# Block-sparse attention and a gated MLP in one kernel: weight parts taken straight from float32, a second weight scaled by halves, merged output products, a new order

## The chip, the core and the metric

One Trainium2 chip, one of its cores. The metric is the device time of one execution in microseconds (us). Engines are named as in the profile: PE (TensorE; PEld is its weight loads), DVE (VectorE), ACT (ScalarE), POOL (GpSimd), SP (SyncE, which here only issues DMAs).

## What is computed

```python
scores = (q @ k.T) / sqrt(64)            # 4 batches, 8 heads, 768 tokens, head size 64
mask   = block neighbours, first and last block of 32 tokens, 3 sampled blocks per block row
attn   = softmax(where(mask, scores, -1e9)) @ v
x      = attn as [3072, 512]
h      = x @ w_in                        # 512 x 2048
g      = h * tanh(softplus(h))
out    = g @ w_out                       # 2048 x 512, float32
```

The two weights arrive as 64-bit floats; the kernel loads them as pairs of 32-bit words and rebuilds float32 from them on DVE ("decoding"). Products are made from 16-bit parts: a number is a high part plus a low part, and of the four products of two such numbers three are kept.

## The kernel before

**Attention.** A batch has 13 jobs: 2 dense ones (the first and the last block row, all keys) and 11 with two block rows each. `attend` records a job: scores S on PE, row maxima on DVE (`mx`), exponentials on ACT (`pt`), transposes T on PE, their parts (`pp`), the products O with v (`o`), division by the row sums on DVE (`xs`), a transpose (`tx`) and the parts of x (`xh`, `xl`). Keys are gathered by POOL and ACT (`kg`), values by DMA from a copy in DRAM (`vg`, SP's queue). Batch 0 is computed in float32, batches 1 to 3 in 16-bit parts. For those `o_fn` (L781) makes, per half of the heads and per 128 keys, twelve matmuls with 32 columns of weights, four beside each other in four column strips: `hi` times v's high part with a column of ones (65 columns), `hi` times v's low part (64), `lo` times v's high part (65), all added into the same place.

**Weights.** w_in comes in eight pieces of 1 MB (`load_i`, ring `wr` of 3 buffers, SP's queue). DVE decodes a piece into the place of its later parts in `wi` (L889, L892, L895); PE multiplies it with itself for the sums of squares (`gram`, L365); from these a power of two is taken as scale (`add_root`). `split_i` (L934) then makes a scaled float32 copy `wt_i` (POOL, ACT or DVE), its high part (ACT) and its low part (POOL, once DVE). The value `gsc`, needed by every h, wants all eight pieces (`scales_w`). w_out comes in 16 pieces of 0.5 MB in the ring `raw`; it has one scale from one gram over all 16 pieces (`scale_o`, 64 matmuls into a bank of the ring `y`), and `parts_o` (L979) makes a copy and two parts of each piece.

**MLP.** For each of 12 tiles of 256 tokens `moe_h` makes h in 16 pieces of 12 matmuls (L1033), `moe_g` the activation on ACT, DVE and POOL, `moe_y` the output in 16 pieces of 6 matmuls (L1093): for each half m of the tile's tokens eight pieces, summed in the one bank of the ring `y`, then scaled into `ys` (L1104 on ACT or L1106 on DVE) and stored. On the last tile m = 0 uses a bank of the ring `h`.

**Order.** Every operation is recorded with `add(engine, duration, ..., key=...)`. `Plan.emit` then writes all engines' programs from these durations, the rings' sizes and the keys: the earliest possible operation goes first, ties by key; the lists START and RES in `pace` hold a job's scores back in favour of the MLP. Up to the tenth job the planner fills the PE gaps that it expects with matmuls on zeros (`zeros`, L868). At run time each engine works through its own fixed list and waits for semaphores.

Of the kernel before, what the change touches and what calls it, by code (L numbers as in the profile page):

```python
# [9 lines left out]
F32 = mybir.dt.float32  # L10
# [10 lines left out]
SQ = 32  # L21
# [5 lines left out]
             xs=2, hs=3, us=3, g=4, ys=1, kt=1, q=2, ssk=2, ssv=2, ssq=2, sck=2, scv=2, scq=2, iv=2, ns=3, ws=2,  # L27
# [158 lines left out]
def attn_mish_kernel(ctx: ExitStack, tc: tile.TileContext, qT, kT, v, sampled, blocks, w_in, w_out, out):  # L186
# [48 lines left out]
    iv_o = const.tile([P, 1], F32, name="iv_o")  # L235
    sc_o = const.tile([P, 1], F32, name="sc_o")
# [4 lines left out]
    gox = const.tile([P, 1], F32, name="gox")  # L241
    hsc = const.tile([P, B], F32, name="hsc")
    osc = const.tile([P, B], F32, name="osc")
# [123 lines left out]
    def add_gram(key, srcs, keys, ring, out, w, new_, cls):  # L367
# [7 lines left out]
        for n, k in enumerate(keys):  # L375
            add("PE", 0.45 if ring == "y" else 0.8, lambda n=n: fn(n), r=[k], w=[kg], new=[(ring, kg)] if n == 0 else (),
                key=cls - 106, lat=0.25)
# [4 lines left out]
        add("DVE", 0.4, diag, r=[kg], w=w, new=new_, key=cls + 5)  # L382
# [20 lines left out]
    def add_root(key, ss, fn, r, after, w, new, cls, n=1, apart=False):  # L403

        add("PE", 0.3 * n, lambda: root_pe(key, ss(), apart), r=r, w=[key], new=[("t", key)], key=cls + 56, lat=0.3)
        add("DVE", 0.65, fn, port=2, r=[key, *after], w=w, new=new, key=cls + 3)

    def load32(what, j):
# [4 lines left out]
        def fn():  # L413
# [5 lines left out]
            key=-5, lat=1.8, kind=("dma", 4.4 if what == "k" else 1.5, 1))  # L419

    def load(b, what, js, ring="raw", after=()):
# [3 lines left out]
        def fn():  # L425
# [12 lines left out]
            new=[(ring, key) for key in keys], key=(-5 if b == 0 else 0) + (0 if b == 0 else 1), lat=1.8,  # L438
            kind=("dma", 1.5 * n, n))

    def sums(b, what, j, cls):
# [7 lines left out]
        add("ACT", 1.28, fn, r=[("raw", what, b, j)], w=[key], new=[(f"ss{what}", key)] if first else (), key=cls + 47 + (19 if b == 0 else 17))  # L449

    def scales(b, what, j, cls):
# [4 lines left out]
        def fn():  # L456
# [14 lines left out]
        add_root(kp, lambda: tl[ks][:, 0:1] if q else tl[ks], fn, [ks], [("sc", "k", b, 0)] if q else [], [key] + ([("ns", b, j)] if q else []),  # L471
                 [(f"sc{what}", key)] + ([("ns", ("ns", b, j))] if q else []), cls, 1 if q else NTT)

    def parts(b, what, j, cls):
# [32 lines left out]
        if what == "v":  # L507
            add("POOL", 0.5, ends, w=[("ends",) + key], r=[kr], new=[("raw", key)], use=[key], key=cls + 2)
# [3 lines left out]
            use=use + ([key] if what != "k" else []), key=cls + 7)  # L512
        add("DVE", 1.27, lo, port=True, r=[kr, ks, kh], w=[key, ("done",) + key], use=use, key=cls - 8)

    def copy_v(j):
# [26 lines left out]
    def globals_(b):  # L542
# [5 lines left out]
        for n in range(NKG):  # L548
            add("POOL", 1.0, lambda n=n: fn(n), r=KT3(b), w=[("kg", n)], use=[("kt", b)], port=2, key=-14)

    def globals_v(b, n):
# [3 lines left out]
        add("SP", 0.9, fn, r=VD3(b), w=[("vg", n)], key=2, lat=1.8, kind=("dma", 0.5, 2))  # L555
# [19 lines left out]
    def gather_k(su):  # L575
# [12 lines left out]
        add("POOL", 1.3, lambda: fn("POOL"), r=KT3(b) + ["off"], w=[("kg", n)], use=[("kt", b)], port=2, key=53 + (7 if b == 0 else 14),  # L588
            also=[("ACT", 1.6 if exact(b) else 1.9, lambda: fn("ACT"))])
        if su["whole"]:  # L590
            add("DVE", 0.36, lambda: nc.vector.tensor_copy(
                out=kgs[n][:, :, 0:WK], in_=tl["kt", b][:, :, (qb - 1) * BS:(qb + 2) * BS]),
                r=KT3(b), w=[("kw", n)], use=[("kt", b)], port=True, key=4)

    def gather_v(su):
# [15 lines left out]
        add("SP", 2.7, fn, r=VD3(b) + ["off", "z"], w=[("vg", n)], key=-18 + (-24 if b == 0 else 0), lat=1.8, kind=("dma", 1.1, NR + 1 + (a0 > 0) + (a1 < WK)))  # L611

    def fetch_dense(su):
# [11 lines left out]
        for j in T3:  # L625
# [3 lines left out]
                key=-3 + (35 if b == 0 else 1), lat=1.8, kind=("dma", 1.7, 1))  # L629
# [32 lines left out]
    def attend(job):  # L662
# [9 lines left out]
        def s_fn():  # L672
# [17 lines left out]
            use=[("kt", b)], key=-39 + (-21 if b == 0 else 20), lat=0.25, kind=("S", i))  # L690
# [12 lines left out]
        add("DVE", 2.6 if dense else 1.27, mx_fn, r=[ks] + (k2 if dense else []), w=[kmx], new=[("mx", kmx)], key=-3.5 + (-1 if b == 0 else -10))  # L703
# [4 lines left out]
        def nb_fn(eng):  # L708
# [9 lines left out]
            new=[("nb", ("nb", i))], key=45.5 + (0 if b == 0 else -20), also=[("DVE", 0.35 * len(wq), lambda: nb_fn("DVE"))])  # L718
# [16 lines left out]
        for n in range(2):  # L735
            add("ACT", 1.7 if dense and n == 0 else 1.15, lambda n=n: ex_fn(n),
                r=[kmx, ("nb", i), ks] + (k2 if dense else []) + NS,
                w=[("p", i, n)], new=[("pt", k) for k in kps] if n == 0 else (), use=kps, key=-1.5 + (-3 if b == 0 else 7))
# [30 lines left out]
        for j in range(nt):  # L769
            kj = ("t", i, j)  # L770
            add("PE", 0.62 if exact(b) else 0.48, lambda j=j: t_fn(j), r=[("p", i, j // 2 if dense else j)], w=[kj, "t in order"], new=[("t", kj)], use=kps,
                key=-8 + (-40 if b == 0 else 24), lat=0.25, kind=("T", i))
            kpp = ("pp", i, j)
            if exact(b):
                add("ACT", 0.62, lambda j=j: pp_fn(j, "ACT"), r=[kj], w=[("ph", i, j), ("pl", i, j)], use=[kpp],
                    new=[("pp", kpp)], key=-9.5, also=[("DVE", 0.72, lambda j=j: pp_fn(j, "DVE"))])
                continue
            add("ACT", 0.62, lambda j=j: ph_fn(j), r=[kj], w=[("ph", i, j)], new=[("pp", kpp)], use=[kpp], key=1.5)
            add("DVE", 0.72, lambda j=j: pl_fn(j), r=[kj, ("ph", i, j)], w=[("pl", i, j)], use=[kpp], key=11.5)

        def o_fn(j):  # L781
            if j == 0:
                new(ps["o"], "o", ko, [P, 2, 2, D + 2])
            o, w = tl[ko], 0 if dense else j
# [11 lines left out]
            for g in range(2):  # L796
                for k in range(2):
# [514 lines left out]
```

## Time and profile before

| | |
|---|---|
| three timed runs | 766.79 us median (765.13 to 769.03) |
| the profiled execution | 768.72 us, of which the span of the core's work 766.7 us |
| busy in the span | PE 733.4, PEld 507.3, DVE 504.0, ACT 535.8, POOL 230.6 us |
| mean granted TensorE clock | 0.99 of full speed |
| HBM traffic | 79.3 MB read, 12.9 MB written |

The span starts with the first instruction and ends with the last. "Busy" is the time in which at least one instruction of the engine was under way; PE's busy time holds the matmuls on zeros too. In a list of waits the last instruction that released a waiting one is named behind "<-".

### The profile page before, as it was taken

The page shows a single profiled execution, that of the slowest core. Times are in us where ns is not written, and L with a number is a line of the kernel's source. Part 1 is how long each engine was busy: PE and PEld are TensorE (multiplying, and loading weights), DVE is VectorE, ACT ScalarE, POOL GpSimd, SP SyncE. Part 2 cuts the span into 40 slices and gives each one's busy share as a digit, 9 for nine tenths or more (in the row PEclk, how much of TensorE's full clock was granted, in tenths as well). Part 3 has the DMA queues.
Part 4 walks back from the last instruction along what each step waited for, and adds up shares of the span by engine and source line. Part 5 has one row for each costly group of instructions (what it writes and reads, how often), then busy time and mean ns, then how long its engine had stood idle before and what let it go on. Part 6 is the DMA issues. An engine that isn't in the chain of part 4 may idle for free.

```text
span 766.7 us, 28001 instructions
## 1 busy us (share of the span) xinstructions
PE 733.4 (96%) x11905; PEld 507.3 (66%) x11905; DVE 504.0 (66%) x891; ACT 535.8 (70%) x864; POOL 230.6 (30%) x327
## 2 busy tenths in 40 slices
PE   9777898999999999999999999999999999999998
PEld 3554676766677766677767776766776666666663
DVE  3886897887888748859676676777855454425241
ACT  2556787989887867888797678877864655455650
POOL 2363423585645422514340113234522100000000
PEclk9999999999999999999999999999999999999999
DMA  7987768442346533543363336233233221000000
GB/s 263 363 222 219 232 210 230 147 128 87 106 120 168 160 96 110 170 123 105 103 210 97 94 100 200 84 97 101 71 92 90 96 67 48 15 15 15 15 15 27
DMA packets 55904, 94.07 MB, mean 123 GB/s; under 512 B 8035, under 2 KB 18788, under 8 KB 55780
## 3 DMA queue, kind: packets, MB, share of 16 engines
q1 hardware_dynamic: 55584, 92.03, 40.0%
q8 instruction: 93, 1.52, 0.8%
q14 instruction: 31, 0.25, 0.1%
q10 hardware_dynamic: 196, 0.27, 0.1%
HBM read 79.32 MB, written 12.95 MB: 120 GB/s over the span
## 4 chain that ended last, share of the span: by engine, by line
PE 82%; DMA 9%; DVE 4%; issue 2%; SPq 2%; ACT 1%; ACTq 0%; POOL 0%
PE y L1093 31%; PE h L1033 30%; PE t L746 6%; PE o L801 5%; PE s L657 4%; DMA wr<-in_moe_w_in_dram 3%; DMA vg<-vd 3%; PE tx L834 2%; PE o L791 1%; DMA wor<-in_moe_w_out_dram 1%; DMA kt<-in_k_dram 1%; PE s L647 1%; PE zeros L868 1%; DMA raw_q<-in_q_dram 1%; DVE us L1060 1%
## 5 line engine op out<-in xcount | busy, mean ns | idle before, releaser
L1033 PE MATMUL h<-xh,wi 128*128 128x256 f16 x1536 | 285.3, 274 | 0.0
L1093 PE MATMUL y<-wo,g 128*128 128x512 f16 x1152 | 277.7, 379 | 1.5 <-issue 1.5
L1033 PEld LDWEIGHTS <-wi 128*128 128x128 f16 x2304 | 224.7, 99 | 52.4 <-issue 1.5
L1033 PE MATMUL h<-xl,wi 128*128 128x256 f16 x768 | 210.5, 274 | 0.0
L1093 PEld LDWEIGHTS <-g 128*128 128x128 f16 x1152 | 111.0, 98 | 101.2 <-issue 3.2
L585 POOL COPY kg<-kt 128x256 f16 (+1 forms) x222 | 97.6, 485 | 145.6 <-PE s L657 115.8
L1042 ACT ACTIVATE hs<-h,gsc 128x512 f32<-128x512 f32 x96 | 65.6, 683 | 63.7 <-PE h L1033 62.9
L726 ACT ACTIVATE pt<-s,nb,ns 128x256 f32<-128x256 f32 (+1 forms) x208 | 105.7, 580 | 5.1 <-PE t L746 3.1
L1066 DVE SCALAR_TENSOR_TENSOR hs<-us,hs 128x1024 f32<-128x1024 f32 x48 | 59.6, 1242 | 43.1 <-ACT us L1065 43.1
L700 DVE TENSOR_REDUCE mx<-s 128x4 f32<-128x1024 f32 x44 | 53.7, 1221 | 31.5 <-PE s L657 30.1
L1077 POOL TENSOR_TENSOR g<-hs,g 128x1024 f16<-128x1024 f32 x19 | 42.3, 2229 | 98.9 <-ACT g L1072 60.2
L746 PE MATMUL t<-ident,pt 128*128 128x128 f32 x448 | 69.5, 278 | 2.0 <-ACT pt L726 1.7
L1062 POOL TENSOR_TENSOR us<-us 128x1024 f32<-128x1024 f32 x22 | 43.4, 1971 | 74.7 <-DVE us L1060 72.2
L766 DVE SCALAR_TENSOR_TENSOR pp<-t,pp 128x512 f16<-128x512 f32 x84 | 56.1, 681 | 11.6 <-ACT pp L763 11.5
L763 ACT ACTIVATE pp<-t 128x512 f16<-128x512 f32 x84 | 48.3, 590 | 17.7 <-PE t L746 13.7
L746 PEld LDWEIGHTS t<-ident,pt 128*128 128x128 f32 x448 | 50.8, 141 | 13.9 <-ACT pt L726 3.2
L1056 ACT ACTIVATE us<-hs,hsc 128x1024 f32<-128x1024 f32 x48 | 55.1, 1149 | 1.5
L1064 ACT ACTIVATE us<-us 128x1024 f32<-128x1024 f32 x48 | 50.7, 1056 | 4.9 <-POOL us L1062 4.1
L1065 ACT ACTIVATE us<-us 128x1024 f32<-128x1024 f32 x48 | 50.7, 1056 | 0.7
L1060 DVE TENSOR_SCALAR us<-us 128x1024 f32<-128x1024 f32 x48 | 36.5, 760 | 21.7 <-ACT us L1056 21.5
L801 PEld LDWEIGHTS <-pp 128*32 128x32 f16 x4032 | 37.2, 94 | 13.7 <-issue 12.3
L852 ACT ACTIVATE xh<-tx 128x256 f16<-128x256 f32 (+1 forms) x60 | 19.4, 337 | 31.4 <-PE tx L834 24.8
(194 smaller groups left out, 849.7 us busy)
## 6 DMA issues: line engine op xcount, KB each, us to landing
vg<-vd SPq DMA_DIRECT2D x304, 65.0 KB, 2.3
vg<-vd SPq DMA_DIRECT2D x80, 195.0 KB, 2.9
wr<-in_moe_w_in_dram SPq DMA_DIRECT2D x8, 1024.0 KB, 9.2
wor<-in_moe_w_out_dram SPq DMA_DIRECT2D x16, 512.0 KB, 5.0
vd<-v SPq DMA_DIRECT2D x12, 520.0 KB, 3.4
raw_v<-in_v_dram SPq DMA_DIRECT2D x12, 512.0 KB, 5.7
out_dram<-ys SPq DMA_DIRECT2D x24, 256.0 KB, 2.1
raw_q<-in_q_dram SPq DMA_DIRECT2D x9, 512.0 KB, 5.5
```

Source lines behind the costliest of these rows:

```text
L585: nc.gpsimd.tensor_copy(out=dst, in_=src)
L700: nc.vector.tensor_reduce(out=mx.rearrange("p g w -> p (g w)"), in_=tl[ks].rearrange("p g (w k) -> p (g w) k", k=KT), axis=AX.X, op=ALU.max)
L726: ex = lambda o, x, g, w: nc.scalar.activation(out=o, in_=x, func=AF.Exp, bias=nb[:, g, w:w + 1], scale=ns(w)[:, 0:1])
L746: nc.tensor.transpose(t[:, k, g], src, ident)
L766: nc.vector.scalar_tensor_tensor(out=tl["pl", i, j], in0=tl["t", i, j], scalar=PSC, in1=tl["ph", i, j], op0=ALU.mult, op1=ALU.subtract)
L801: nc.tensor.matmul(o[cs, w, g, 0:v1 - v0], p[:, k, g, cs], vt[:, k, 2 * c + g, v0:v1], start=j == 0 and g == 0 and k == 0 and n == 0, stop ...
L1033: nc.tensor.matmul(h[:, f2].rearrange("p (s q) -> p s q", q=BS), wi[:, fp, w, cc, fs], x[:, :, cc], start=f2 == 0 and k == 0, stop=f2 == 1 ...
L1042: nc.scalar.activation(out=tl[kq][:, 2 * (fp % 2):2 * (fp % 2) + 2], in_=tl[kh], func=AF.Copy, scale=gsc[:, fp:fp + 1])
L1056: nc.scalar.activation(out=new(sb, "us", ku, [P, 4, TT]), in_=hs(), func=AF.Exp, scale=hsc[:, b:b + 1])
L1064: add("ACT", 1.07, lambda: nc.scalar.activation(out=us(), in_=us(), func=AF.Ln, bias=1.0), w=[ku], key=10 + (18 if b == 0 else -12))
L1066: add("DVE", 1.32, lambda: nc.vector.scalar_tensor_tensor(out=hs(), in0=us(), scalar=-0.5, in1=hs(), op0=ALU.add, op1=ALU.mult), r=[ku], w ...
L1093: nc.tensor.matmul(tl[ky], tl["g", b, t, k][:, g, f, q], wo[:, fc, w], start=fc == 0 and n == 0, stop=fc == NFC - 1 and n == 2)
```

## The change

It has five parts.

- **w_in.** A decoded piece now goes into a buffer of the rings `us` or `hs` (`at_i`) instead of its place in `wi`. Both parts are made from there: the high part by ACT (or DVE), the low part by one SCALAR_TENSOR_TENSOR on DVE. The scaled copy is gone, and POOL has no part in it.
- **w_out.** Two scales, one for each half of the 16 pieces. The sums of squares come from ACT (`squares`, 16 times) instead of PE's gram. The parts are stored one place on along a chain, so that each is made straight from the decoded piece; only the first high part of a half waits in a buffer.
- **y.** `moe_y` sums each half (two of four k) by itself: 48 sums of 24 matmuls instead of 24 of 48. The first of a pair goes to `ys` scaled, the second is added to it by DVE. `ys` has two buffers. On the last tile the first halves use the ring `h`, the second ones the one bank of `y`.
- **O of batches 1 to 3.** `hi` meets v's high and low part in one matmul of 130 columns for the first three of the four (block row, half of heads) places; the low part's sum lies elsewhere in the bank, is copied out (`xc`) and added on DVE.
- **Sums of k and v squares (batches 1 to 3)** are added on DVE before PE, which then multiplies one column instead of three. **Keys, RES and START** all have other values; v of batch 0 is loaded ahead of k and q.

```diff
-RINGS = dict(... ys=1 ...)
+RINGS = dict(... ys=2 ...)
...
-        add_root(kp, lambda: tl[ks][:, 0:1] if q else tl[ks], fn, ...)
+        three = not q and b == 0
+        if not q and b:
+            add("DVE", 0.2, lambda: nc.vector.tensor_reduce(out=tl[ks][:, 0:1], in_=tl[ks], axis=AX.X, op=ALU.add), r=[], w=[ks], key=cls - 37)
+        add_root(kp, lambda: tl[ks] if three else tl[ks][:, 0:1], fn, ...)
...
-                    for n, (p, v0, v1) in enumerate(((hi, 0, D + 1), (hi, D + 1, 2 * D + 1), (lo, 0, D + 1))):
+                    steps = ((hi, 0, VW, slice(m, m + 5, 4)), (lo, 0, D + 1, m)) if m < 3 else (
+                        (hi, 0, D + 1, m), (hi, D + 1, 2 * D + 1, m), (lo, 0, D + 1, m))
...
+                nc.vector.tensor_tensor(out=xs[:, 0:m], in0=o[:, 0:m, 0:D], in1=xs[:, 0:m], op=ALU.add)
+                nc.vector.tensor_tensor(out=xs[:, 0:m], in0=xs[:, 0:m], in1=rb[:, 0:m].to_broadcast([P, m, D]), op=ALU.mult)
...
+            add("ACT", 0.35, lambda: xc_fn("ACT"), r=[ko], w=[("xc", i)], new=[("xs", ("xs", i))], key=52,
+                also=[("DVE", 0.3, lambda: xc_fn("DVE"))])
...
     def a0_i(k):
-        return wi[:, k].rearrange("p t c f -> p (t c f)").bitcast(F32)
+        return tl["a0", k]
+
+    def at_i(k):
+        ring = ("us", "hs")[k % 2]
+        return [(ring, ("a0", k))], lambda: new(sb, ring, ("a0", k), [P, 4 * TT])
...
-        add("POOL", 1.4, lambda: t_fn("POOL"), r=[ksc, ("wi", k)], w=[kt], new=[("raw", kt)], ...
-        add("ACT", 1.1, lambda: nc.scalar.activation(out=hi, in_=tl[kt], func=AF.Copy), r=[kt], ...
-        add("POOL", 2.1, lambda: nc.gpsimd.tensor_tensor(out=lo, in0=tl[kt], in1=hi, op=ALU.subtract), ...
+        add("ACT", 1.16, lambda: nc.scalar.activation(out=hi, in_=a0_i(k), func=AF.Copy, scale=sc()), r=[ksc, ("wa", k)], ...
+        add("DVE", 1.27, lambda: nc.vector.scalar_tensor_tensor(out=lo, in0=a0_i(k), scalar=sc(), in1=hi, op0=ALU.mult, op1=ALU.subtract), ...
...
-    def scale_o(cls):
-        add_gram(("wo",), [lambda fc=fc: a0_o(fc) for fc in range(NFC)], [("wo", fc) for fc in range(NFC)], "y", ...
+    NHO = 2
+    NFH = NFC // NHO
+    chain = [[h * NFH + (n - 1) % NFH for n in range(NFH)] for h in range(NHO)]
+    before = {c: cs[n - 1] for cs in chain for n, c in enumerate(cs)}
+
+    def wo_of(fc, w):
+        return wo[:, before[fc], 1] if w == 0 else wo[:, fc, 0]
+
+    def scale_o(h, cls):
+        for fc in fcs:
+            add("ACT", 0.65, lambda fc=fc: ss(fc), r=[("oa", fc)], w=[("am1", fc)], ...
...
-        pool = "h" if last and m == 0 else "y"
+        h = k // KH
+        pool = "h" if last and h == 0 else "y"
...
+            if h:
+                nc.vector.scalar_tensor_tensor(out=ys, in0=tl[ky], scalar=sc, in1=ys, op0=ALU.mult, op1=ALU.add)
...
-        ys = [(m, k) for m in range(TT // P) for k in range(NFC // 4)] if prev else []
+        ys = [(m, h * KH + k) for h in range(NHO) for m in range(TT // P) for k in range(KH)] if prev else []
...
-    RES, START = 518, [19, 70, 50, 10, 634, 35, 526, 50, 20, 45, 52, 127, 40, 172, 123, 69, 17, 154]
+    RES, START = 493, [300, 706, 46, 26, 320, 3, 1101, 1150, 300, 903, 90, 104, 101, 108, 1204, 183, 158, 49]
```

Some 60 keys change as well; what they do shows in the order of the engines' programs. Three places of it follow. In the names `h_b_t_n` is piece n of h for batch b, tile t; `o_i`, `s_i`, `t_i`, `tx_i` belong to job i.

PE ahead of the first h, before:

```order
L746 MATMUL t_5_1_1337<-ident_64,pt_5_1261 128x128 x4
...
L365 MATMUL gram_wo_1347<-wo_72 128x128
...
L647 MATMUL s_6_1358<-kt_0_123,q_0_1_167 32x96 x8
L647 MATMUL s_6_1358<-kg0_109,q_0_1_167 32x160 x8
...
L834 MATMUL tx_4_1410<-ident_64,xs_4_1402 128x128 x2
...
L1033 LDWEIGHTS wi_71
L1033 MATMUL h_0_0_0_1444<-xh_0_0_607,wi_71 128x256
```

and now:

```order
L749 MATMUL t_6_1_1464<-ident_64,pt_6_1368 128x128 x4
L650 MATMUL s_7_1478<-kt_0_163,q_0_1_167 32x96 x8
...
L866 MATMUL tx_4_1519<-ident_64,xs_4_1514 128x128 x2
...
L796 MATMUL o_5_1550<-vg0_111,pp_5_0_1227 32x65 x16
...
L796 MATMUL o_5_1550<-vg1_112,pp_5_1_1321 32x65 x16
L749 MATMUL t_7_0_1637<-ident_64,pt_7_1601 128x128 x4
L1087 LDWEIGHTS wi_71
L1087 MATMUL h_0_0_0_1647<-xh_0_0_533,wi_71 128x256
```

The first h now stands behind one job's scores, one job's O and three T groups more; one group of the gram of w_out is gone from there. All zeros stand ahead of it in both programs: 139 before, 160 now.

SP at the loads of w_in (`wr`) and the first gathers of values, before:

```order
L881 DMA wr_4_469<-in_moe_w_in_dram 128x4x512
L554 DMA vg0_111<-vd0_60 32x520 x2
L554 DMA vg1_112<-vd0_60 32x520 x2
L881 DMA wr_5_557<-in_moe_w_in_dram 128x4x512
L604 DMA vg0_111<-vd0_60 64x520
...
L604 DMA vg1_112<-vd0_60 96x520
...
L881 DMA wr_6_763<-in_moe_w_in_dram 128x4x512
L604 DMA vg0_111<-vd0_60 96x520
```

and now:

```order
L913 DMA wr_5_476<-in_moe_w_in_dram 128x4x512
L557 DMA vg0_111<-vd0_60 32x520 x2
L557 DMA vg1_112<-vd0_60 32x520 x2
L913 DMA wr_6_651<-in_moe_w_in_dram 128x4x512
L607 DMA vg0_111<-vd0_60 64x520
...
L607 DMA vg1_112<-vd0_60 96x520
...
L913 DMA wr_7_825<-in_moe_w_in_dram 128x4x512
L607 DMA vg0_111<-vd0_60 96x520
```

Pieces 5, 6 and 7 of w_in each moved ahead by the gathers of one job.

DVE in the last tiles, around the sums of y that go to `ys` (tile 1 of batch 3), before:

```order
L1066 SCALAR_TENSOR_TENSOR hs_3_2_0_15838<-us_3_2_0_15882,hs_3_2_0_15838 128x1024
L1106 TENSOR_SCALAR ys_3_1_0_15981<-y_3_1_0_15810,osc_82 128x512
L1060 TENSOR_SCALAR us_3_2_1_15966<-us_3_2_1_15966 128x1024
L1066 SCALAR_TENSOR_TENSOR hs_3_2_1_15925<-us_3_2_1_15966,hs_3_2_1_15925 128x1024
L1079 TENSOR_TENSOR g_3_2_0_16029<-hs_3_2_0_15838,g_3_2_0_16029 128x1024
L1074 CAST g_3_2_1_16072<-hs_3_2_1_15925 128x1024
```

and now:

```order
L1133 TENSOR_TENSOR g_3_1_3_14847<-hs_3_1_3_14741,g_3_1_3_14847 128x1024
L1168 TENSOR_SCALAR ys_3_1_0_14890<-y_3_1_0_0_14803,osc_82 128x512
L1114 TENSOR_SCALAR us_3_2_0_14875<-us_3_2_0_14875 128x1024
L1120 SCALAR_TENSOR_TENSOR hs_3_2_0_14831<-us_3_2_0_14875,hs_3_2_0_14831 128x1024
L1128 CAST g_3_2_0_14937<-hs_3_2_0_14831 128x1024
L1133 TENSOR_TENSOR g_3_2_0_14937<-hs_3_2_0_14831,g_3_2_0_14937 128x1024
L1168 TENSOR_SCALAR ys_3_1_1_14980<-y_3_1_1_0_14893,osc_82 128x512
```

Each tile's output now empties the bank of `y` four times instead of twice, and each time directly behind a DVE operation on 1024 columns.

## Rows read from the trace of the kernel before

**Rows 1.** The page's busy times of two engines.

```profile
PE 733.4 (96%) x11905; PEld 507.3 (66%) x11905; DVE 504.0 (66%) x891; ACT 535.8 (70%) x864; POOL 230.6 (30%) x327
```

**Rows 2.** Busy time of each engine in three stretches of the span.

```profile
0.00:135.00 135.00, 112.69 (x1906) 75.65 (x1910) 101.09 (x198) 84.04 (x156) 51.33 (x71) 0.96 0.80 249
135.00:300.00 165.00, 164.89 (x2969) 116.77 (x2958) 128.60 (x230) 138.41 (x230) 82.95 (x103) 1.00 0.42 125
...
78.60:141.00 62.40, 55.79 (x1004) 44.19 (x1002) 51.36 (x106) 48.26 (x85) 21.07 (x25) 0.95 0.73 218
```

**Rows 3.** PE's matmuls on zeros, from the groups by form.

```profile
L868 PE MATMUL zeros<-z 128*128 128x512 f16 x139 | 35.7, 400 | 5.6 <-issue 3.9 <-POOL z L863 1.7
```

**Rows 4.** The first h, from PE's timeline.

```profile
81.23 0.27 PE L1033 MATMUL h<-xh,wi 128*128 128x256 f16 x1
```

**Rows 5.** PE's waits in the whole span, the one that the gram of w_out makes.

```profile
PE gram_wo L365 <- DVE wo L895: 3.6, 3, 3.1
```

**Rows 6.** Groups of that gram in PE's timeline.

```profile
90.55 0.39 PE L365 MATMUL gram_wo<-wo 128*128 128x128 bf16 x4
90.78 0.60 PE L746 MATMUL t<-ident,pt 128*128 128x128 f32 x4
...
95.81 0.41 PE L365 MATMUL gram_wo<-wo 128*128 128x128 bf16 x4 [3.06 <-DVE wo L895]
96.05 0.63 PE L746 MATMUL t<-ident,pt 128*128 128x128 f32 x4
```

**Rows 7.** O of a dense and of a two-row job, and what followed, PE's timeline.

```profile
203.11 1.36 PE L801 MATMUL o<-v,pp 128*32 128x65 f16 x144
204.40 0.66 PE L746 MATMUL t<-ident,pt 128*128 128x128 f32 x4
...
219.48 1.01 PE L801 MATMUL o<-vg,pp 128*32 128x65 f16 x96
220.42 0.66 PE L746 MATMUL t<-ident,pt 128*128 128x128 f32 x4
```

**Rows 8.** The last piece of a sum of y, an h piece, the next sum: PE's timeline.

```profile
719.95 1.46 PE L1093 MATMUL y<-wo,g 128*128 128x512 f16 x6
721.25 0.27 PE L1033 MATMUL h<-xh,wi 128*128 128x256 f16 x1
...
722.56 1.46 PE L1093 MATMUL y<-wo,g 128*128 128x512 f16 x6
```

**Rows 9.** The emptying of that bank, DVE's timeline.

```profile
721.45 0.75 DVE L1106 TENSOR_SCALAR ys<-y,osc 128x512 f32<-128x512 f32 x1 [4.60 <-PE y L1093]
```

**Rows 10.** Three columns of squares added on PE, its timeline.

```profile
137.00 0.73 PE L391 MATMUL tp_k<-ss_k,ones 128*128 128x1 f32 x6
```

**Rows 11.** Parts of one job of batch 0 in PE's timeline.

```profile
84.88 0.40 PE L647 MATMUL s<-kt,q 64*32 64x96 f32 x16
...
86.02 0.66 PE L746 MATMUL t<-ident,pt 128*128 128x128 f32 x4
86.61 0.66 PE L791 MATMUL o<-vg,pp 128*32 128x65 f32 x32
87.20 0.66 PE L746 MATMUL t<-ident,pt 128*128 128x128 f32 x4
```

**Rows 12.** DVE's groups by form that the change adds to or takes from.

```profile
L1066 DVE SCALAR_TENSOR_TENSOR hs<-us,hs 128x1024 f32<-128x1024 f32 x48 | 59.6, 1242 | 43.1 <-ACT us L1065 43.1
...
L1060 DVE TENSOR_SCALAR us<-us 128x1024 f32<-128x1024 f32 x48 | 36.5, 760 | 21.7 <-ACT us L1056 21.5
...
L500 DVE SCALAR_TENSOR_TENSOR v<-raw_v,sc_v,v 128x1024 f16<-128x1024 f32 x9 | 11.6, 1304 | 1.5 <-ACT v L496 1.5
```

**Rows 13.** Issues of w_in's pieces 5, 6 and 7 in SP's timeline.

```profile
33.62 0.38 SPq L881 DMA_DIRECT2D wr<-in_moe_w_in_dram  x1
...
44.36 0.45 SPq L881 DMA_DIRECT2D wr<-in_moe_w_in_dram  x1
...
53.21 0.40 SPq L881 DMA_DIRECT2D wr<-in_moe_w_in_dram  x1
```

More of the change, by code (lines that the diff above doesn't have):

```diff
@@ L448, in fn @@
             squares(tl["raw", what, b, j], tl[key][:, k:k + 1])
[L449 removed]
+        add("ACT", 1.28, fn, r=[("raw", what, b, j)], w=[key], new=[(f"ss{what}", key)] if first else (), key=cls + 47 + (41 if b == 0 else -6))
     def scales(b, what, j, cls):
@@ new lines, in parts_o @@
+        add("ACT", 0.65, lambda: h_fn("ACT"), r=[("sc_o", h), ("oa", fc)] + ([] if first else [("wol", before[fc])]),
+            w=[("woh", fc)] + ([kt] if first else []), new=[("raw", kt)] if first else (), key=cls - 31, port=True,
+            also=[("DVE", 0.45, lambda: h_fn("DVE"))])
+        add("DVE", 0.69, lambda: nc.vector.scalar_tensor_tensor(out=lo, in0=a0_o(fc), scalar=sc, in1=to(), op0=ALU.mult, op1=ALU.subtract),
+            r=[("sc_o", h), ("oa", fc), kt if first else ("woh", fc)], w=[("wol", fc)], port=True, key=cls - 32)
@@ L997, in scales_w @@
+        if last:
+            c0 = chain[h][0]
+            src = lambda: tl["wt", c0]
+            add("ACT", 0.6, lambda: nc.scalar.activation(out=wo_of(c0, 0), in_=src(), func=AF.Copy), r=[("wt", c0), ("wol", fc)],
+                w=[("woh", c0)], key=cls + 11, port=True, also=[("DVE", 0.35, lambda: nc.vector.tensor_copy(out=wo_of(c0, 0), in_=src()))])
     def scales_w():
@@ new lines, in moe_y, with ys_fn @@
+        if k % KH < KH - 1:
+            return
+        def ys_fn(eng):
+            if h == 0:
+                new(pools["m"], "ys", kys, [P, DM])
+            ys, sc = tl[kys], osc[:, b, h:h + 1]
+            if h:
+                nc.vector.scalar_tensor_tensor(out=ys, in0=tl[ky], scalar=sc, in1=ys, op0=ALU.mult, op1=ALU.add)
+            elif eng == "ACT":
+                nc.scalar.activation(out=ys, in_=tl[ky], func=AF.Copy, scale=sc)
+            else:
+                nc.vector.tensor_scalar(out=ys, in0=tl[ky], scalar1=sc, scalar2=None, op0=ALU.mult)
@@ new lines, in out_fn @@
+        def out_fn():
+            r0 = b * S + t * TT + m * P
+            nc.sync.dma_start(out=out[r0:r0 + P, :], in_=tl[kys])
+        add("DVE", 0.76, lambda: ys_fn("DVE"), r=[ky, ("osc", b, h)] + ([("ysw", b, t, m, 0)] if h else []),
+            w=[("ysw", b, t, m, h)], new=[("ys", kys)] if h == 0 else (), use=[kys], key=4 + (4 if b == 0 else -17),
+            also=[("ACT", 0.7, lambda: ys_fn("ACT"))] if h == 0 else ())
+        if h == NHO - 1:
+            add("SP", 0.4, out_fn, r=[("ysw", b, t, m, h)], use=[kys], key=2 + (-15 if b == 0 else -83), lat=1.8, kind=("dma", 0.8, 1))
```

272 lines of the change are left out of this document (143 added, 129 removed).

## The prediction

> **What bounds the kernel now.** I read the page's busy times first. There the reader is to see that PE is busy in 96% of the span, DVE in 66%, ACT in 70% and POOL in 30% [rows 1]: over the whole, PE is the bound. Then the engines by stretch. From 135 to 300 us PE is busy in 164.89 of 165 us, at the full clock; from 0 to 135 us in only 112.69, so 22.3 us are idle there [rows 2], and 35.7 us of the busy part are matmuls on zeros [rows 3], all of them ahead of the first h at 81.23 us [rows 4]. So there are two stages. In the first, PE waits for weights, gathers and vector work; what it is given there may cost nothing, and what it is spared may bring nothing. In the second, every PE microsecond is a microsecond of the end, and other engines count only where they make PE wait. PE's timeline late in that stage shows the beat of the MLP: a y piece of 6 matmuls from 719.95 to 721.25 (1.30 us), then 12 matmuls of h to 722.56 (1.31 us), and no gap [rows 8].
>
> The profiled execution took 768.72 us with a span of 766.7, 2.0 us around it and 1.9 us above the median. Each term below comes from that span; I put the sum on the median of 766.79.
>
> **The change part by part.**
>
> *Gram of w_out.* The order takes 64 matmuls in 16 groups from PE. A group runs from 90.55 to 90.78, .23 us [rows 6]; 16 give 3.7 us. They lie between 78.6 and 141 us, where PE is busy in 55.79 of 62.40 us, 89% [rows 2]; taking that share as what counts, **-3.3** (ends 0, if gaps take it up, and -3.7). Their waits on the decoded pieces are 3.6 us in 3 places, the longest 3.06 at 95.81 [rows 5, 6]. No PE instruction reads w_out before the first y now, so I take all: **-3.6** (ends 0, if the next PE instruction waits as long for something else, and -3.6). In exchange ACT squares 16 pieces and DVE makes more low parts, off PE's path.
>
> *Merged O.* Per place the matmuls fall from three in a group of four strips to two for three places of four: the order has 1080 fewer matmuls, 270 groups. The columns hardly change (65 + 64 + 65 becomes 130 + 65, one more). The price of a group by the rows: a dense job's 144 matmuls (36 groups) take 1.29 us (203.11 to 204.40), a two-row job's 96 (24 groups) .94 us (219.48 to 220.42) [rows 7]; the difference is .35 us for 12 groups, 29.2 ns each. Columns alone: a y piece moves 6 x 512 in 1.30 us [rows 8], .423 ns a column, so 65 columns are 27.5 ns. What a group costs beside its columns is then 1.7 ns, and 270 of them **-.5**. Ends: 0; and, from the .94 us over all 24 groups, 39 ns each, 11.7 above its columns, -3.1. I take the difference, since the larger figure holds the start of a job's O too, which stays. [...] The additions that take the place (a copy out and two operations on DVE for each job) hang off the same O; the DVE of this stage has room by the row below.
>
> *Root sums.* Three columns of squares take .73 us on PE, .24 each [rows 10]. The order has 11 of these fewer (6 for v, 6 for k, one more for w_out): 11 x .24 = **-2.7**, from the batches where PE is full (ends 0 and -2.7).
>
> *Tail.* The last tile's two second halves share the one bank of y. PE must wait between them until the bank is emptied: that starts .20 us after the matmuls (721.25 to 721.45) and takes .75 [rows 8, 9]: **+1.0** (ends 0, if the last products don't directly follow, and 1.0).
>
> *Turns of the y bank, 24 before and 48 now.* A sum's bank is free again at 722.20, and the next sum starts at 722.56 behind an h piece [rows 8, 9]. The slack is .36 us, so I cost 24 more at **0**; this holds only while DVE or ACT takes the bank at once (a rival below).
>
> *DVE and ACT.* DVE gets 24 more operations on y, 8 low parts of w_in of about 1.30 us (as one of v, the nearest form [rows 12]) and 16 of w_out, and the parts of the merged O; ACT loses the copies of both weights and gets the squares. Between 135 and 300 us DVE is busy in 128.60 of 165, 78%, while PE never waits [rows 2]: costed at **0**, covered by PE's own work. If that cover goes, the price is the rival's.
>
> *The ramp.* Ahead of the first h now stand one more job's scores (84.88 to 86.02, 1.14 us), one O (two halves of .59) and three T groups (.59 each) [rows 11], less one group of the gram (.23). That is 1.14 + 1.18 + 1.77 - .23 = 3.9 us that no longer has to be done later; and 21 more zeros of 512 columns, at .423 ns a column .217 us each, 4.5 us if no gap were there to hold them. If the work falls into idle time the ramp gives -3.9; if the zeros overfill it, +4.5. These are the two ends; since the same planner put both where it expects idle time, I take **0**. Loading v ahead of k and q delays the first scores, while PE has nothing but zeros.
>
> The sum: -3.3 - 3.6 - .5 - 2.7 + 1.0 = -9.1, so 766.8 - 9.1 = 757.7, about **758**. With all best ends 766.8 - 3.7 - 3.6 - 3.1 - 2.7 - 3.9 = 749.8; with all worst 766.8 + 1.0 + 4.5 = 772.3.
>
> **The rivals.**
>
> *R1, h starts earlier.* Every h needs the scale that wants all eight pieces of w_in. The SP order has pieces 5, 6 and 7 each one job's gathers earlier; before, they were issued at 33.62, 44.36 and 53.21 us, so such a step is worth some 9 to 11 us of issue time [rows 13]. If the loads are what the first h waits for, and DVE decodes them as they come, h could start about 7 us sooner (I take three quarters of 9), and take the place of zeros and of idle time: 757.7 - 7 = **751**. Against it: DVE has 101.09 us of work in the first 135 [rows 2], about as much as now by the order, and gathers that stand behind a 1 MB load come later.
>
> *R2, the ramp hides the gram.* Between 78.6 and 141 us PE has 6.6 us idle with the gram in it [rows 2]. If those gaps are set by chains over DVE, ACT and DMA (maxima, exponentials, gathers), then taking matmuls and one kind of wait from PE only makes it wait for the next thing: -3.3 and -3.6 go, and **764.6** is left, no change. For it: DVE is at 51.36 of 62.40 us there, and the new low parts of w_out come to it. Against it: 3.06 us of the wait stand in one place, ahead of transposes that were ready at once.
>
> *R3, the turns of the y bank are exposed (slower).* The y ring has one bank. In DVE's order each of the new emptyings stands behind an operation on 1024 columns, of .76 us (`us`) or 1.24 (`hs`), mean 1.00 [rows 12]. If such a one has just begun when the sum is complete, the bank comes free that much later: 1.00 - .36 of slack = .64 us, in each of 24 new turns 15.4 us, 757.7 + 15.4 = **773**. It decides as soon as the operation in front has more than .36 us left on the average. Against it: in the last tiles DVE idled 4.60 us before it emptied the bank [rows 9]; through most of the program it has a quarter of its time free. [...]
>
> **How the numbers follow.** The forecast has .40, R1 .17, R2 .25, R3 .18. A measurement of this kernel can tell about 0.5% from no change, that is 763.0 to 770.6 count as the same. The forecast and R1 are faster, .57; R2 is the same, .25; R3 slower, .18. The range goes from 747, R1 with a little of the best ends, to 775, R3 with 2 us to spare; outside are the best ends of R1 and an R3 in which turns of before are exposed as well. The forecast's own range is 750 to 764.
>
> **What would show it.** Right: PE's busy time falls by 5 to 8 us, apart from zeros; PE's idle time from 80 to 140 us falls by about 3 us; the beat of y and h stays at 2.6 us, also over a turn of the y bank; the first h starts between 78 and 84 us; between the last two sums stands about 1 us. R1: the first h before 76 us. R2: the first y no earlier than before, and in the list of waits PE's transposes or O in the place of the gram's 3.6 us. R3: waits of PE's y on DVE or ACT `ys`, of some tenths of a us each and many of them. If merged O takes as long as before less .12 us per job, the price of a group is wrong too. Wrong altogether: PE idle in the steady stage, from 140 us on, by more than 2 us, for any other cause (a low part of w_out or of w_in that comes late, or the copies of O).

## The result, and the profile after

Four runs of the changed kernel took 755.99 us (median; 755.78 to 760.0), four of the kernel before 766.5 (765.13 to 769.03). The ratio is 0.9872, with a 95% interval of 0.983 to 0.9913: faster by 1.3%, 10.5 us. The forecast was 758. The sum came out right by luck: two of its terms were wrong, one too large and one too small, and they made up for each other.

Two lines of the page after, PE's busy time and the packets of the queue that carries instructions:

```profile
PE 727.2 (96%) x10760; PEld 499.0 (66%) x10760; DVE 547.0 (73%) x1035; ACT 543.1 (72%) x887; POOL 207.8 (28%) x319
...
q8 instruction: 84, 1.38, 0.8%
```

The second line on the page before:

```profile
q8 instruction: 93, 1.52, 0.8%
```

PE has 6.2 us less to do [rows 1] although its zeros grew by 5.5 [rows 3]; DVE has 43 us more. PE's instructions, a weight load and a matmul each, are 2 x 11905 before and 2 x 10760 after; over 93 and 84 packets that is 256 instructions a packet both times (the second trace of the changed kernel has 85 packets), 16.4 KB each; with the 182 and 195 semaphore and drain instructions that the traces hold beside them, PE's instructions are 93.7 and 84.8 times 256. So by these counts q8 carries PE's program, in pieces of 256 instructions. The prediction did not look at this line.

The stretches after (columns as in [rows 2], PE first):

```profile
78.60:141.00 62.40, 54.05 (x1047) 40.75 (x1048) 48.86 (x101) 46.65 (x93) 16.90 (x28) 0.97 0.74 212
135.00:300.00 165.00, 161.68 (x2617) 113.82 (x2616) 144.83 (x278) 141.98 (x236) 66.65 (x86) 1.00 0.43 125
300.00:500.00 200.00, 199.85 (x3288) 141.17 (x3286) 162.49 (x316) 160.72 (x259) 79.42 (x112) 1.00 0.44 128
500.00:700.00 200.00, 200.00 (x2633) 139.68 (x2632) 121.16 (x213) 136.75 (x206) 32.92 (x50) 1.00 0.22 64
```

The last two stretches before, which the prediction had not read:

```profile
300.00:500.00 200.00, 196.37 (x3746) 140.06 (x3752) 142.65 (x263) 159.01 (x257) 60.90 (x101) 1.00 0.43 126
500.00:700.00 200.00, 196.53 (x2925) 137.20 (x2922) 111.38 (x180) 125.28 (x192) 35.45 (x54) 1.00 0.23 66
```

Before, PE was idle for 3.6 and 3.5 us there, in the stage that the prediction called full; after, for 0.15 and 0. From 78.6 to 141 us it is the other way: PE now idles 8.4 us, where it was 6.6 [rows 2]; up to 78.6 us it idles 12.5, where it was 15.7.

PE's waits after (total us, times, longest):

```profile
PE o L796 <- DMA vg<-vd: 7.9, 9, 2.6
PE o L796 <- issue: 3.1, 2, 2.6
PE tp_v L391 <- ACT I-186_187 L356: 2.2, 1, 2.2
...
PE y L1151 <- DVE ys L1164: 0.9, 1, 0.9
...
PE y L1151 <- ACT ys L1166: 0.3, 1, 0.3
```

PE's waits before, besides that of the gram [rows 5]:

```profile
PE o L791 <- DMA vg<-vd: 6.6, 9, 2.1
...
PE o L801 <- issue: 3.2, 2, 1.7
...
PE y L1093 <- issue: 1.5, 1, 1.5
PE s L657 <- issue: 1.4, 1, 1.4
```

"issue" means that nothing in the profile held the matmul. Four such stalls, 6.1 us, stood after the first y before; none does after, where all that are left lie in the ramp (the two of O above, one of S of 1.2 us and one of .4). The two waits of y on the emptying of its bank are all that 48 turns cost.

Four places on PE's timeline after: the first h, the first y, O of a two-row job with the transpose behind it, and the last turn of the y bank:

```profile
88.74 0.27 PE L1087 MATMUL h<-xh,wi 128*128 128x256 f16 x1
...
147.16 0.59 PE L1151 MATMUL y<-wo,g 128*128 128x512 f16 x2
...
352.15 0.91 PE L812 MATMUL o<-vg,pp 128*32 128x130 f16 x72
352.99 0.33 PE L749 MATMUL t<-ident,pt 128*128 128x128 f32 x1
...
742.08 1.46 PE L1151 MATMUL y<-wo,g 128*128 128x512 f16 x6
744.45 1.24 PE L1151 MATMUL y<-wo,g 128*128 128x512 f16 x5 [0.91 <-DVE ys L1164]
```

The first y before:

```profile
145.11 0.39 PE L1093 MATMUL y<-wo,g 128*128 128x512 f16 x1
```

The first h comes 7.5 us later than before [rows 4], the first y 2.1 us later. The gain lies wholly behind the first y: from it to the last matmul of y it is 617.5 us before and 602.3 now. The two profiled executions are 12.9 us of span apart, the medians 10.5 us, so what follows overstates the gain by some 2 us.

Where PE's time went, each matmul counted from its start to the next one's, and only what lies past a matmul's end as idle (summed over the whole timelines of the first trace of each kernel, us):

| | before | after | difference |
|---|---|---|---|
| idle until the first y | 20.6 | 19.1 | -1.5 |
| zeros | 34.4 | 39.5 | +5.1 |
| gram of w_out | 4.4 | 0 | -4.4 |
| O | 57.9 | 53.4 | -4.5 |
| root sums of v, k and w_out | 4.7 | 2.0 | -2.8 |
| idle after the first y | 7.2 | 1.8 | -5.4 |
| all else | 631.6 | 631.9 | +0.3 |

The ramp is not the same from one execution to the next: in the second traces the idle time until the first y is 16.9 us before and 17.2 after.

### The profile page after: what moved, and what is told of

It reads as the page before. It is cut to its first block, busy times and chain, and to the rows that moved or that the text cites. A ratio compares the mean times of both kernels' runs of the same rounds, so it can differ in the third digit from the quotient of the medians.

```text
span 753.8 us, 25872 instructions
## 1 busy us (share of the span) xinstructions
PE 727.2 (96%) x10760; PEld 499.0 (66%) x10760; DVE 547.0 (73%) x1035; ACT 543.1 (72%) x887; POOL 207.8 (28%) x319
## 4 chain that ended last, share of the span: by engine, by line
PE 80%; DMA 7%; DVE 7%; SPq 3%; issue 1%; ACT 1%; DVEq 0%; ACTq 0%
PE y L1151 32%; PE h L1087 31%; PE t L749 6%; PE o L812 4%; PE s L660 4%; DMA vg<-vd 3%; DMA wr<-in_moe_w_in_dram 2%; PE tx L866 1%; DVE mx L703 1%; PE s L650 1%; DMA raw_k<-in_k_dram 1%; SPq L613 1%; DMA wor<-in_moe_w_out_dram 1%; PE o L796 1%; DVE a L926 1%
## 5 line engine op out<-in xcount | busy, mean ns | idle before, releaser
L588 POOL COPY kg<-kt 128x256 f16 (+1 forms) x234 | 104.5, 490 | 193.6 <-PE s L660 126.5
L1116 POOL TENSOR_TENSOR us<-us 128x1024 f32<-128x1024 f32 x26 | 50.3, 1934 | 76.6 <-DVE us L1114 74.8
L703 DVE TENSOR_REDUCE mx<-s 128x4 f32<-128x1024 f32 x44 | 53.4, 1213 | 8.1 <-PE s L660 4.2
L1131 POOL TENSOR_TENSOR g<-hs,g 128x1024 f16<-128x1024 f32 x19 | 41.5, 2182 | 63.2 <-ACT g L1126 26.8
L1164 DVE SCALAR_TENSOR_TENSOR ys<-y,osc,ys 128x512 f32<-128x512 f32 x24 | 17.9, 747 | 36.5 <-PE y L1151 36.4
L900 PE MATMUL zeros<-z 128*128 128x512 f16 x160 | 41.2, 403 | 2.1 <-POOL z L895 1.7
L1133 DVE TENSOR_TENSOR g<-hs,g 128x1024 f16<-128x1024 f32 x29 | 37.9, 1305 | 4.4 <-ACT g L1126 3.8
```

The lines of the kernel that those rows point to most:

```text
L588: nc.gpsimd.tensor_copy(out=dst, in_=src)
L703: nc.vector.tensor_reduce(out=mx.rearrange("p g w -> p (g w)"), in_=tl[ks].rearrange("p g (w k) -> p (g w) k", k=KT), axis=AX.X, op=ALU.max)
```

## The experiments

Two theories were held against each other. That of the prediction: the gram and its waits are the gain, merging O saves next to nothing. The rival, from the table: the ramp gave the gram's time back, in zeros or in other waits, and the gain comes from O, by a price for each matmul and by stalls of PE's program. Where an order is kept, every instruction stands where it stood; only what is named differs. Times are medians. The runs were made in three groups, each beside the kernel before: it took 767.3 us beside the runs with pieces cut elsewhere, the even gram and the old lists, and 766.0 us beside the others. The lines of code below are shortened.

### The two kernels again

No edit.

> The kernel before once more, for a second trace. In its first trace PE idles 7.2 us after the first y, 6.1 of them in four stalls without a releaser (466, 498, 519 and 616 us). If they come from how the program is loaded, stalls of this size return, with the places near bursts of short matmuls; if they were an accident of one execution, less than 2 us idle remain and the time is about 763 us.

> The changed kernel once more, for a second trace of it and as the base of the runs beside it. If PE's few stalls without a releaser (82.8, 107.3 and 136.1 us) belong to the program, they come back at the same places; if they belong to one execution, some are elsewhere or gone. Time 754 to 758 us by either.

The kernel before took 765.96 us; its stalls on PE's timeline, in the second trace:

```profile
465.35 0.59 PE L1093 MATMUL y<-wo,g 128*128 128x512 f16 x2 [1.19 <-issue]
...
497.70 0.51 PE L657 MATMUL s<-kg,q 64*32 64x256 f16 x20 [1.38 <-issue]
...
517.97 0.46 PE L801 MATMUL o<-vg,pp 128*32 128x65 f16 x35 [1.45 <-issue]
...
614.51 0.24 PE L801 MATMUL o<-vt,pp 128*32 128x64 f16 x8 [1.25 <-issue]
```

They came back at the same four places, 5.3 us together. The same matmul is held each time: after 28 matmuls of S in a job of 48, after 61 of O in 96. They belong to the program, not to one execution. The changed kernel took 756.4 us (754.66 to 757.46), again without a stall of this kind after the first y (idle 1.6 us there). In its first trace three stood in the ramp, from 82.7, 94.5 and 136.0 us on (the one expected at 107.3 has a gather as its releaser). None of the three came back as a stall without a releaser; at 139.2 us O waited for a gather instead. A fourth, of .4 us before a matmul on zeros (75.2 us), came back at the same matmul with 1.7 us.

### O with the merge undone

```diff
-steps = ((hi, 0, VW, slice(m, m + 5, 4)), (lo, 0, D + 1, m)) if m < 3 else (
+steps = ((hi, 0, D + 1, m), (hi, D + 1, VW, m + 4), (lo, 0, D + 1, m)) if m < 3 else (
...
```

> The changed kernel in its own order, with each merged matmul of 130 columns made as two of 65 again (1080 more matmuls, the same columns). The prediction's theory (a group of four costs 1.7 ns beside its columns): +0.5 us over the changed kernel, +3.1 at its far end. Rival, from PE's time by tile in the two traces (O after the first y 41.4 us before and 37.0 now): 16 ns for each of 270 groups, +4.4 us, and on top of it stalls of PE without a releaser of 1.2 to 1.7 us each, since PE's program comes in 16 KB pieces of 256 instructions and is used up faster: in all +5 to +10 us.

It took 762.56 us (760.76 to 765.7), 6.2 over the changed kernel beside it; ratio to before 0.9955 (0.9939 to 0.9972), against 0.9868 (0.9841 to 0.9895). After the first y, O took 41.5 us in place of 37.0: 4.5 us for 270 groups, 16.6 ns each. Idle time there rose from 1.8 to 5.2 us, most of it in new stalls, the largest two:

```profile
233.68 1.24 PE L1149 MATMUL y<-wo,g 128*128 128x512 f16 x5 [0.87 <-issue]
...
349.44 0.27 PE L1085 MATMUL h<-xl,wi 128*128 128x256 f16 x1 [1.57 <-issue]
```

Both stand shortly behind an O. The rival's numbers hold, the prediction's (+.5, at most +3.1) do not. By the medians 6.2 of the 9.6 us beside this run, more than half of the gain, are the merge of O.

### y in matmuls of 256 columns

```diff
-nc.tensor.matmul(tl[ky], ..., wo_of(fc, w), ...)
+for c in range(2):
+    cs = slice(c * DM // 2, (c + 1) * DM // 2)
+    nc.tensor.matmul(tl[ky][:, cs], ..., wo_of(fc, w)[:, cs], ...)
```

> The changed kernel in its own order, with each y matmul of 512 columns made as two of 256 (1152 more matmuls, about as many as the merge of O took away, but where 256 instructions last some 14 us). If a matmul had a fixed price of its own of some 15 ns or more, +17 us or more; if columns alone count, 0 to +1 us. If stalls of PE's program depend on how fast its instructions are used up and not on their number, no stall without a releaser over 1 us is added after the first y.

It took 758.28 us (757.57 to 760.5), 1.9 more. The time of y rose from 251.3 to 254.4 us: 3.1 us for 1152 more matmuls, 2.7 ns each. Idle time after the first y was 2.0 us, with one stall of .5. As many matmuls as O lost, put where 256 instructions last about 14 us (128 of the 2304 matmuls that take 254.4 us), bring no stall of the size of before. Beside its columns, the runs show 2.7 ns for a matmul on the whole array and 16.6 ns / 4 = 4.2 ns for one of O.

### The gram left out

```diff
-gram(tl[kg], srcs[n](), n == 0, n == len(srcs) - 1)
+if ring != "y" or n in (0, len(srcs) - 1):
+    gram(tl[kg], srcs[n](), n == 0, n == len(srcs) - 1)
```

> The kernel before in its own order, with 14 of the 16 groups of the gram of w_out left out on PE (only the first and the last piece are summed, so w_out gets another scale). The prediction's theory: 14/16 of 3.3 us of matmuls and of 3.6 us of waits go, -6.0 us. Rival (the ramp hides the gram): PE waits for gathers and transposes instead, idle time before the first y rises by what the gram took, 0 to -2 us.

Neither: 769.75 us (765.94 to 773.38), ratio 1.0046 (1.0017 to 1.0075). The kernel with 56 matmuls fewer was slower. Two of its waits tell where:

```profile
PE h L1034 <- issue: 5.0, 3, 2.5
PE tx L835 <- ACT hs L1043: 4.7, 1, 4.7
```

The first y came at 143.9 us, between those of the two traces of the kernel before (145.1 and 143.2): a transpose waits 4.7 us for ACT in one place, where the gram's longest waits were 3.1 and 2.0. And after the first y idle time is 10.2 us instead of 7.2 and 6.2, in stalls at other places than before (316, 351, 393 us among them). With 112 instructions of PE gone, every later piece of 256 is cut at another instruction.

### The gram left out, the program as long as before

Beside the edit above:

```diff
-nc.tensor.matmul(<zeros, 512 columns>)
+for x in range(2 if <one of the first 56 zeros> else 1):
+    nc.tensor.matmul(<zeros, 256 or 512 columns>)
```

> The kernel before with 14 of 16 groups of the gram of w_out left out, as in the run few_gram, and as many matmuls put in early: 56 of the matmuls on zeros are made as two of 256 columns. PE's program has its length of before again, so from the gram on its pieces of 256 instructions are cut where they were cut before. If the 3.8 us that few_gram lost come from where the pieces are cut: PE's stalls after the first y are the four of before (some 5 to 6 us, at about 464, 496, 516 and 613), and the time shows what the gram itself is worth: -6.0 by the prediction's theory, 0 to -2 by the rival that the ramp hides it. If few_gram lost them in another way (a colder ramp, other data): 768 us or more again.

767.79 us (762.78 to 772.66), ratio 1.0005 (0.9979 to 1.0031): no change; a gain of more than 1.6 us lies outside the interval. On PE's timeline stand the wait in the ramp and the first of the stalls:

```profile
97.47 0.66 PE L835 MATMUL tx<-ident,xs 128*128 128x128 f32 x2 [4.97 <-ACT hs L1046]
...
464.77 0.59 PE L1097 MATMUL y<-wo,g 128*128 128x512 f16 x2 [1.75 <-issue]
```

What PE's wait in the ramp goes back to stands on DVE. In the kernel before, and in this run:

```profile
94.12 0.43 DVE L889 TENSOR_SCALAR wo<-wor 128x512 int32<-128x512 int32 x1 [3.47 <-DMA wor<-in_moe_w_out_dram]
...
90.56 0.43 DVE L893 TENSOR_SCALAR wo<-wor 128x512 int32<-128x512 int32 x1 [2.81 <-DMA wor<-in_moe_w_out_dram]
...
94.56 0.30 ACT L714 ACTIVATE nb<-mx,ns 128x4 f32<-128x4 f32 x1 [3.35 <-DVE mx L701]
```

Both times DVE stands still until a piece of w_out has landed, then decodes it. Before, the gram waited for that decoding. Without the gram the same delay reaches PE another way: the row maxima stand behind the decoding in DVE's program, ACT waits for them with its exponentials, and the transpose waits for what follows those on ACT and DVE.

The stalls after the first y are back at the four places of before (463, 496, 516 and 613 us, 5.6 us). So the gram by itself was worth nothing that this run could tell. PE's 3.8 us less of gram stand against 4.4 us more of idle time ahead of the first y beside the second trace of the kernel before, but 3.6 against .7 beside the first; executions differ by as much there, so it is the ratio that decides. That the cut of the pieces made few_gram slower rests on the traces; the intervals of the two ratios overlap.

### Pieces cut elsewhere

64 of the early zeros split in the same way, in each kernel, and nothing else.

```diff
-nc.tensor.matmul(<zeros, 512 columns>)
+for x in range(2 if <one of the first 64 zeros> else 1):
+    nc.tensor.matmul(<zeros, 256 or 512 columns>)
```

> The kernel before in its own order, with 64 of the early matmuls on zeros made as two of 256 columns: the same work, and every later instruction of PE stands 128 places, half a piece, further on. If stalls come where a piece of the program arrives late in a burst of short matmuls, they stand at other places than 464, 496, 516 and 613 us and their sum changes, anything from 1 to 12 us, the time with it by -4 to +6. If they belong to these places of the work: the same four, and the time within 1 us of before.

> The changed kernel in its own order, with the same shift by 64 split matmuls on zeros. If the changed kernel's freedom from stalls after the first y is partly a matter of where its pieces are cut: stalls of 1 to 2 us appear there, 1 to 6 us more. If it comes from the merge alone (fewer instructions in the bursts): idle time after the first y stays under 2 us, time 754 to 758.

In the kernel before the four stalls vanished, and seven others came; the four largest:

```profile
207.18 0.74 PE L657 MATMUL s<-kg,q 64*32 64x256 f16 x39 [1.08 <-issue]
...
267.38 0.30 PE L801 MATMUL o<-vg,pp 128*32 128x65 f16 x15 [0.75 <-issue]
...
351.76 0.36 PE L801 MATMUL o<-v,pp 128*32 128x65 f16 x23 [1.69 <-issue]
...
395.51 0.28 PE L1036 MATMUL h<-xl,wi 128*128 128x256 f16 x1 [1.52 <-issue]
```

These lie in or shortly behind S and O, and the sum of the seven happens to be the same (5.8 us, where the two traces of the kernel before have 6.1 and 5.3); the time is 768.06 us, ratio 1.0006 (0.9978 to 1.0033). The changed kernel got one stall in the last two of 48 matmuls of S:

```profile
355.01 0.28 PE L660 MATMUL s<-kg,q 64*32 64x256 f16 x2 [0.94 <-issue]
```

It took 757.53 us (756.34 to 759.79), ratio 0.9889 (0.9857 to 0.9921), with 2.8 us idle after the first y. Where the pieces are cut decides which bursts stall; how much they stall is less with fewer matmuls in a burst: .0 to 2.4 us after the first y in the eight traces with O merged, 3.6 to 7.5 us in the six with O in three matmuls. That the stalled matmul waits for its piece shows when PE's weight loads, matmuls and semaphore instructions are counted in the traces. All 33 stalls without a releaser after the first y (those over .15 us), in the fourteen traces of this case, stand at the same place of a piece, 192 or 193 instructions past a multiple of 256, and a packet of the instruction queue had ended 1.26 to 1.52 us before each; of 43 waits with a releaser one stands there (1.3 us before S, in the kernel with the gram left out). In the first trace of the kernel before the four stand 193 past, a multiple of 256 from each other, and 1.35 to 1.52 us after a packet. A piece of 256 instructions, 128 matmuls, lasts about 1.25 us in O (96 in .94 us [rows 7]) and 14 us in h (.11 us each). That a burst uses up its pieces faster than they come is an estimate from these numbers; no run changed how they are loaded.

### Half the zeros

```diff
-nc.tensor.matmul(..., z16, z16.unsqueeze(1).to_broadcast([P, 4, P]), ...)
+nc.tensor.matmul(..., z16, z16.unsqueeze(1).to_broadcast([P, 2, P]), ...)
```

> The changed kernel in its own order, with each of the 160 matmuls on zeros over 256 instead of 512 columns, some 17 us less of zeros. The prediction's theory (filler where PE waits anyway): the time stays within 1 us, and idle time before the first h rises by about what the zeros lose. Rival (21 more zeros overfill the gaps and delay the first h): the first h comes 2 to 5 us sooner and the time falls by as much. Third: the granted clock falls below 0.9 somewhere before 150 us and the time rises.

755.72 us (754.29 to 756.28), ratio 0.9858 (0.9815 to 0.9901): within 1 us of the changed kernel. The zeros took 15 to 17 us less than in the two traces of the changed kernel, and idle time before the first h rose by 11 to 12; the first h came at 89.4 us (88.7 and 91.2 with full zeros). The granted clock did fall: its mean over an execution was .978 to .983 of full speed in the four runs, .986 to .995 in eight of the changed kernel, and the time did not rise with it. The stretch from 60 to 90 us does not show this by itself; here and in the second trace of the changed kernel, with full zeros, it is nearly the same (.95 in the first):

```profile
60.00:90.00 30.00, 24.47 (x507) 17.62 (x488) 22.53 (x55) 21.86 (x47) 4.65 (x15) 0.79 0.74 218
...
60.00:90.00 30.00, 24.92 (x417) 15.03 (x409) 22.00 (x55) 21.19 (x45) 4.24 (x14) 0.80 0.69 196
```

So the zeros are filler, as the prediction had it, and the 5 us more of them cost nothing that the run could tell. What sets the ramp's end is other engines and transfers.

### The root sums thrice

```diff
-nc.tensor.matmul(tp, ones, ss[:, k:k + 1], ...)
+for _ in range(3):
+    nc.tensor.matmul(tp, ones, ss[:, k:k + 1], ...)
```

> The changed kernel in its own order, with each of the six one-column sums of v and k squares of batches 1 to 3 made three times on PE (same result; the additions on DVE stay). The prediction's theory: 12 more columns of .24 us on a full PE, +2.9 us. Rival: those sums stand where PE waits for the roots anyway, 0 to +1 us.

PE's time for these sums rose by 2.7 us, 2.2 of it after the first y, as the prediction costed them. The time is 757.32 us (753.82 to 759.33), ratio 0.9878 (0.9841 to 0.9915): 0.9 to 1.3 us over the changed kernel's medians, too little to tell 2.7 from 1.

### Another bank for the last sum

```diff
-pool = "h" if last and h == 0 else "y"
+pool = "h" if last and (h == 0 or m == 1) else "y"
```

> The changed kernel with the second of the last tile's second halves in a bank of the ring of h instead of the bank of y. The prediction's term for the tail (PE waits between the last two sums for the bank to be emptied): the .91 us gap at the last turn goes, -0.9 us. Rival (the end is set by the last emptying and the store, or the new bank is itself still in use): 0.

The gap of .91 us is gone from PE's timeline. The time is 755.42 us (752.24 to 758.43), ratio 0.9864 (0.9826 to 0.9903): the lowest median of all, but a microsecond lies inside its interval.

### The old lists in the new kernel

```diff
-RES, START = 493, [300, 706, 46, 26, ...]
+RES, START = 518, [19, 70, 50, 10, ...]
```

> The changed kernel with the two lists RES and START of the kernel before, which hold back the scores of each job; all engines' orders follow from them. The prediction took 0 for the new order: within 2 us of the changed kernel. Rival: the new lists carry part of the gain in the steady stage: 3 to 10 us slower, with PE waiting for maxima, exponentials or gathers after the first y.

765.27 us (762.52 to 771.34), ratio 0.9977 (0.9946 to 1.0008): the gain is all but gone. The profiled execution is the slowest of the ten (771.34 us). In it the first y comes at 141.5 us, 5.7 earlier, and then idle time is 11.5 us instead of 1.8. One wait on the squares of q is half of it. From 187 to 192 us, behind these 5.8 us without a matmul, the granted clock is .55 of full speed; from 200 to 300 us it is 1.00:

```profile
PE tp_q L391 <- ACT I-3344_3345 L356: 5.8, 1, 5.8
```

```profile
187.00:192.00 5.00, 4.44 (x72) 2.09 (x73) 4.96 (x3) 4.33 (x7) 4.05 (x2) 0.55 0.29 108
```

The new kernel needs lists of its own. That is not the same as a gain from the new order: both kernels have lists that fit them, and this run says what misfitting ones cost. The kernel before with the new lists was not run. It also shows that an earlier first y is no gain by itself.

## Why the prediction was right, and where not

- **The whole.** 755.99 us lies in the range (747 to 775), in the forecast's own (750 to 764) and 2 us from the forecast. The sum of terms was -9.1; measured are -10.5. That they are so near is luck, as the next two terms show. Two of the signs that the prediction named came out otherwise: PE's busy time apart from zeros fell by 11.7 us and not by 5 to 8, and its idle time from 80 to 140 us rose from 6.1 to 8.3 us and did not fall by 3.
- **Gram and waits, -6.9: wrong.** The step that failed is "No PE instruction reads w_out before the first y now, so I take all". With 14 of its 16 groups left out and nothing else moved, the gram is worth 0 (ratio 1.0005, at most 1.6 us). PE waited for something else in the same stretch, in one place of 5 us, as the second rival said of the ramp. The chain is the one which that rival named: a late piece of w_out, DVE's decoding and maxima, ACT's exponentials. The prediction took the wait for the gram's own, while it was the wait of DVE's whole program for that piece.
- **Merged O, -.5: mis-sized, by far.** The step that failed is the price of a group beside its columns, 1.7 ns. It is 16.6 ns, -4.5 us, above the far end of 11.7 as well. A column price from a matmul on the whole array was put on matmuls in strips, and the difference of two jobs was taken for the cost of a group. And the term had no place for the stalls: undoing the merge brought 3.4 us of idle time after the first y. The prediction's own alarm (O shorter by about .12 us in a job) rang: .94 before [rows 7], 352.15 to 352.99 = .84 now.
- **PE's time after 135 us, taken as full: wrong for the later part.** The statement rested on 135 to 300 us [rows 2]. 6.1 us of stalls lay between 466 and 616.
- **Root sums, -2.7: right in PE's time** (4.7 to 2.0); what of it reaches the end the run could not resolve.
- **Tail, +1.0: right**, .91 us.
- **Turns of the y bank, 0: right.** PE waits .26 us at one of them besides the last. The third rival did not happen: DVE and ACT got to the bank in time, although DVE is busier by 43 us. How much later they could come was not tried.
- **Ramp, 0: right as a cost, wrong in the place of the first h.** It starts at 88.74 us, outside the 78 to 84 named, with the first y 2.1 us later. The first rival (h earlier by the loads of w_in) fell: the last two pieces are issued 5 us earlier, at 39.4 and 48.3 us, and h starts later all the same. It stands behind more work in PE's order; the zeros are not the reason, since with half of them it came no sooner.
- **Zeros as filler: right.**

With the gram at 0, O at -6.2 and the other terms as they were, the sum is -6.2 - 2.7 + 1.0 = -7.9. The 2.6 us that are left have no run of their own; the new order, which moved S and T ahead of the first h, is the part of the change that was not separated. By the same count as in the table, 3.6 us of h, S, T and tx have moved from behind the first y to ahead of it, which is nearly the 3.9 us that the prediction set as the ramp's good end; but the first y comes 2.1 us later in the first pair of traces and 5.3 in the second. Whether a part of the 2.6 us lies there is open.

## What to carry to other kernels

Where an engine has gaps, price an instruction that you take out by what stands behind the next wait, not by its own time: the gram's matmuls and waits, priced at 6.9 us, were worth nothing that a run could tell. Follow such a wait back to its start, past the engine that released it: the next instruction may be waiting for the same thing. Read the waits of the full stage to its end, those without a releaser too: the long program here stood still for 6.1 us at four fixed places of its instructions, in or behind bursts of short matmuls, and 1080 matmuls fewer in the bursts were worth 6.2 us with about the same columns. When a small edit moves the time the wrong way, look at whether stalls of this kind have moved before looking for a reason in the work.

## What had not been expected of the hardware

**PE's program comes in pieces, and late at times.** 256 instructions a packet (2 x 11905 over 93, 2 x 10760 over 84); stalls of .2 to 2.5 us, all in bursts of S and O or within 2.7 us behind one, always at the same place of a piece (192 or 193 past a multiple of 256), that move to other matmuls when 112 or 128 instructions are put in or taken out ahead. In the two traces of the kernel before they are 6.1 and 5.3 us after the first y.

**Changing between the whole array and strips.** An h matmul takes .11 us until the next h starts, and .20 us until an S does:

```profile
207.66 0.27 PE L1087 MATMUL h<-xl,wi 128*128 128x256 f16 x1
207.77 0.27 PE L1087 MATMUL h<-xh,wi 128*128 128x256 f16 x1
207.97 0.85 PE L660 MATMUL s<-kg,q 64*32 64x256 f16 x48
```

In both traces, after 150 us, every step from h, t or tx to S or O is .20 us and nearly every one to h, y, t or tx is .11; after y it is .31 and .22. That is .09 us for each of some 80 entries, about 7.5 us in either kernel. The way out costs as much again: from the last matmul of S, which has 256 columns as one of h has, to the next h it is .20 us too. No run changed the shape of the matmuls alone, so what the .09 us come from is not shown.
